# Decayed attention and a GELU MLP in one program: where the loads, the attention steps and the copies of waves 0 to 2 stand, and the last block in two halves

## The chip, the cores and the metric

The kernel runs on one core of a Trainium2 chip. The metric is device time in microseconds (us) of one launch: the median of several runs. One more execution is profiled; its span is the time from the first to the last instruction that the profiler saw.

Engines: PE (TensorE, matmuls into PSUM), DVE (VectorE), ACT (ScalarE), POOL (GpSimd), SP (SyncE, which here only issues DMAs). Each engine works through its own queue in order, and semaphores hold an instruction until what it needs is done. A DMA that SP or POOL issues is carried out by 16 DMA engines that all queues share.

## What is computed

Four sequences of 768 positions, eight heads of 64. In blocks of 64 positions a linear attention with a decay `lam` per head is computed, with a state `kv_state` that goes from block to block; the result, as 3072 rows of 512, goes through a two-layer MLP.

```python
for b in range(nb):                                    # nb = 768 // 64
    intra = np.einsum('bhic,bhjc->bhij', qb, kb) * Dmask[None]
    intra = np.einsum('bhij,bhjd->bhid', intra, vb)
    inter = np.einsum('bhid,bhde->bhie', qb * lam_pow[None], kv_state)
    out[:, :, sl] = intra + inter
    kv_state = lam_block[None, :, None, None] * kv_state + np.einsum('bhsd,bhse->bhde', kb_dec, vb)
...
h = x @ w_in                                           # 512 -> 2048
g = h * (1.0 / (1.0 + np.exp(-1.702 * h)))
return (g @ w_out).astype(np.float32)                  # 2048 -> 512
```

## The kernel before

**Waves.** The work is cut into six waves of 512 rows (`NW` = 6). Waves 0 and 1 are "big": two of the four sequences each, 256 positions at once. Waves 2 to 5 take 128 positions of all four sequences. Heads go in four pairs, p = 0 to 3. A wave's attention gives four tiles `xT` (one for each pair, 128 x 512, bf16), which are the MLP's input, transposed.

**MLP.** `mlp1(w, fc, kcs)` (L371) makes one 128 x 512 tile of the hidden layer out of four matmuls, over the four `xT` tiles, and ACT writes its GELU to `g_sb` (L381). `mlp2(w, g, j)` (L383) makes four of the 16 matmuls of one block of 128 output rows; the last of the four j copies the block on DVE to `o_sb` (L392) and stores it through SP (L394). A call of either is one item of the list `main`, four matmuls with 512 columns each; the first nine items of waves 0 and 1 are cut up differently (three tiles begun on the first two pairs, then one matmul each for the third and the fourth pair).

**Attention of a big wave.** `big_cast` (L219) multiplies k or q by a decay and casts it to bf16, on DVE or POOL as the call says; `big_cast_v` (L227) casts v on POOL; `big_t` (L232) transposes k and q of one pair on PE and copies both out of PSUM on ACT (L242); `big_s` (L245) makes the scores; `big_m` (L259) masks them on DVE (L262); `big_kv` (L268) makes the states of two pairs, which ACT copies to `mid` and `first` (L283, L284); `big_st` (L287) combines them on DVE; `big_c` (L294) makes the output of one pair, and ACT copies it to `xT` (L311).

**Attention of waves 2 to 5.** `do_cast` (L193) scales k and q on DVE (L199, L200), casts v on POOL, and has k and q transposed by a DMA on SP's queue (L205). `scores` (L314) makes the scores of two pairs on PE (L321) and masks them on DVE (L325); `mix` (L348) makes their output and the new state.

**Order.** All engines' orders follow the order in which the program is written out. The prologue up to L474 is written by hand: wave 0's attention, filler matmuls on a tile of zeros between its steps (`fill`, L215), loads of the weights on POOL's queue (`w_in` in five chunks, then `w_out` in four, cast to bf16 on the way), and on SP's queue, behind a wait, the loads of waves 1 and 2. That wait is `sync_behind_weights` (L186): SP copies four bytes out of `w_out_sb[2]`, the third of the four chunks, so that nothing behind it on SP's queue is issued before that chunk has landed. From L475 on, `main` is the list of MLP items of all waves, and `side` is a list of attention steps with due positions: a step is written out ahead of the first item whose index is not below its position (L490 to L494). Wave 0 has items 0 to 37 (22 of `mlp1`, then 16 of `mlp2`, the first eight of them in turns over two blocks, chunk after chunk of `w_out`), wave 1 items 38 to 75. The list `BIG` (L399) gives the positions of wave 1's attention. For a later wave w + 1 they are n + 1 + 2p for the casts and n + `SCORES_AT`, n + `MIX_AT` for scores and mix (L484 to L486), with n = 44 for wave 2.

**PSUM.** Eight banks: three with the tag "mm" (`ps_h`, `ps_out` and, in wave 0, the transposes of `big_t`) and five with the tag "att" (all other attention tiles). `bank(..., mm)` (L209) picks the tag. A tile of a tag waits until the tile that had its buffer has been read.

Of the kernel before, what the change touches and what calls it, by code (L numbers as in the profile page):

```python
# [24 lines left out]
def kernel(  # L25
# [13 lines left out]
    nc = tc.nc  # L39
    f32 = mybir.dt.float32  # L40
    bf16 = mybir.dt.bfloat16
    B, H, S, D = q.shape
    P = 128
# [27 lines left out]
    NB = 2  # L71
# [76 lines left out]

    def more_consts():
        nc.scalar.activation(inv_pow, ln_lam, EXP, scale=i_inv)  # L150
        for h in range(2):
            hs = slice(64 * h, 64 * h + 64)
            nc.scalar.activation(blk_pow[hs], ln_lam[hs].rearrange("p (n h) -> p n h", h=2)[:, :, h], EXP, scale=i_blk[hs])

    def last_consts():
        for x, i in ((k_pow, i_k), (q_pow, i_q)):
            nc.scalar.activation(x, ln_lam, EXP, scale=i)

# [26 lines left out]

    def sync_behind_weights():  # L186

        nc.sync.dma_start(out=behind, in_=w_out_sb[2][0:1, 0, 0:2])


    cast, trans, masked, xT, g_of, h_ps, o_ps, vbig, sc_of, kv_of = ({} for _ in range(10))
# [37 lines left out]
        nc.gpsimd.tensor_copy(vb, pair_of(w, "v", p))  # L229
        vbig[w, p] = vb  # L230

    def big_t(w, p, q_out=None):  # L232
        kq = work.tile([P, 2, BB, 2, P], bf16, tag=f"kq{p}", name="kqB")
        for i, nm in enumerate("kq"):
            ps_t = bank([P, BB, 2, P], bf16, f"ps_t{nm}", w == 0)
            for bb in range(BB):
                for t in range(2):
                    nc.tensor.transpose(ps_t[:, bb, t, :], cast[w, p][:, i, bb, t, :], ident)  # L238
            if nm == "q" and q_out is not None:
                q_out.tensor_copy(kq[:, i], ps_t)  # L240
            else:
                nc.scalar.copy(kq[:, i], ps_t)  # L242
        trans[w, p] = kq
# [127 lines left out]
    def mlp1(w, fc, kcs):  # L371
# [8 lines left out]
        if kcs[-1] == KC - 1:  # L380
            nc.scalar.activation(g_of[w][:, fc, :], h_ps.pop(fc), GELU)  # L381

    def mlp2(w, g, j):  # L383
        if j == 0:
            o_ps[w, g] = ps.tile([P, d_model], f32, tag="mm", bufs=3, name="ps_out")
        ps_out = o_ps[w, g]
        for fc in range(j * CW, (j + 1) * CW):
            nc.tensor.matmul(ps_out, g_of[w][:, fc, g * P : (g + 1) * P], w_out_sb[j][:, fc % CW, :],  # L388
                             start=(fc == 0), stop=(fc == FFC - 1))
        if j == FFC // CW - 1:  # L390
            o = op.tile([P, d_model], f32, tag="o", name="o_sb")
            nc.vector.tensor_copy(o, ps_out)  # L392
            r0 = (BB * w + g // 2) * S + (g % 2) * P if w < NB else g * S + w * P
            nc.sync.dma_start(out=out[r0 : r0 + P, :], in_=o)  # L394

    EARLY = 3
    SCORES_AT, MIX_AT = (13, 21), (19, 27)
    V, G_ = nc.vector, nc.gpsimd
    BIG = [(27, big_cast, "k", 0, V), (27, big_cast, "q", 0, G_), (27, big_cast, "k", 1, V), (27, big_cast, "q", 1, G_),  # L399
           (30.5, big_cast, "k", 2, V), (30.5, big_cast, "k", 3, V), (30.5, big_cast_v, 0), (30.5, big_cast_v, 1),  # L400
           (31, big_t, 0), (32, big_t, 1), (33, big_s, 0), (33, big_m, 0), (34, big_s, 1), (34, big_m, 1),
           (34, big_kv, 0, False), (34, big_st, 0), (34, big_cast, "q", 2, G_), (34, big_cast, "q", 3, V),
           (35.5, big_c, 0), (35.5, big_c, 1), (36.5, big_t, 2), (36.5, big_t, 3), (37, big_s, 2), (37, big_m, 2),
           (37.5, big_s, 3), (37.5, big_m, 3), (37.5, big_cast_v, 2), (37.5, big_cast_v, 3), (38, big_kv, 2, False),
           (41, big_c, 2), (41, big_c, 3, 0, V.tensor_copy), (41, big_st, 2)]
    first, last = list(range(KC - 1)), [KC - 1]

    def mlp2_items(w):

        nj = FFC // CW  # L410
        if w == 0:
            return ([(mlp2, w, g, j) for j in range(nj) for g in range(2)]
                    + [(mlp2, w, g, j) for g in range(2, G) for j in range(nj)])
        return [(mlp2, w, g, j) for g in range(G) for j in range(nj)]

    def mlp_items(w):
# [7 lines left out]
    with tc.manual_schedule():  # L424
# [5 lines left out]
        big_cast(0, "q", 0, G_)  # L430
        big_t(0, 0)
        more_consts()
        last_consts()
        big_cast(0, "k", 1, V)
        big_cast(0, "q", 1, G_)
        big_s(0, 0, 3)
        big_m(0, 0)
        big_t(0, 1)
        nc.scalar.preload_act_table(GELU)
        big_s(0, 1, 2)  # L440
        big_m(0, 1)
# [3 lines left out]
        load_w_in(1)  # L445
        big_kv(0, 0, False, 3)
        big_cast(0, "k", 2, V)
        big_c(0, 0, 6)
        big_c(0, 1, 8)
        big_cast(0, "q", 2, G_)  # L450
        load_w_in(2)
        load_w_in(3)
        big_cast(0, "k", 3, V)
        big_cast(0, "q", 3, V)
        big_st(0, 0)
        big_t(0, 2)
        big_t(0, 3)
        big_s(0, 2, 2)
        big_m(0, 2)
        big_s(0, 3, 1)  # L460
# [15 lines left out]
        for w in range(NW):  # L476
            n = len(main)
            main += mlp_items(w)
            e = len(main)
            if w == 0:  # L480
                side += [(at, (f, 1, *a)) for at, f, *a in BIG]
            elif w + 1 < NW:
                n = e - FFC - len(mlp2_items(w))
                side += [(n + 1 + 2.0 * p, (do_cast, w + 1, p)) for p in range(NP)]  # L484
                for i, ps2 in enumerate(([0, 1], [2, 3])):
                    side += [(n + SCORES_AT[i], (scores, w + 1, ps2)), (n + MIX_AT[i], (mix, w + 1, ps2))]  # L486
            if w and w + 2 < NW:
                side += [(n + 8, (load, w + 2))]
        side.sort(key=lambda x: x[0])
# [35 lines left out]
```

## Time and profile before

| | us |
|---|---|
| median of 3 runs | 218.73 (218.3 to 218.84) |
| the profiled execution | 218.17 |
| its span | 216.5 |
| PE busy in the span | 203.1 |
| ACT, DVE, POOL busy | 87.3, 84.8, 31.9 |
| first w_out matmul of wave 0 on PE | 33.67 |
| last matmul's copy on DVE begins | 212.70 |

A line of the timeline gives start, length, engine, line of the kernel, operation, output and inputs, and how many instructions were merged into it; the bracket is the engine's idle time just before and what ended it. "SPq" is SP issuing DMAs. A line of the chain of waits gives start, length and what the end of the program hung on at that time. In lines of groups, the two numbers behind the bar are the busy time and the mean of one instruction in ns. A line on landing gives the time from the issue of a DMA to its data being there. The PEclk row of the slices is the clock that TensorE was granted, in tenths.

### The profile page before, as it was taken

What the parts mean: (1) busy time and instruction counts of PE and PEld (TensorE: products, weight loads), DVE (VectorE), ACT (ScalarE), POOL (GpSimd) and SP (SyncE); (2) the same over time, 40 slices, a digit from 0 to 9 for tenths busy, and PEclk for the clock granted to TensorE, in tenths of its full rate; (3) what the DMA queues carried; (4) which work ended last, traced back from release to release, by engine and by line L of the source; (5) the groups of instructions that cost most, each with busy time, mean ns of one, the idle gap of its engine ahead of it and who ended that gap; (6) DMA issues with size and microseconds to landing.
All of it is one profiled execution on the core that took longest, in us unless ns stands there. A gap on an engine that the chain in (4) does not pass through costs nothing.

```text
span 216.5 us, 4280 instructions
## 1 busy us (share of the span) xinstructions
PE 203.1 (94%) x1721; PEld 100.5 (46%) x1747; DVE 84.8 (39%) x187; ACT 87.3 (40%) x164; POOL 31.9 (15%) x60
## 2 busy tenths in 40 slices
PE   7789999988897999999999999999999999999992
PEld 2465444545443455444545444545444545444440
DVE  2687000585853173442283533282624061100121
ACT  4784772236664311166311275301366301476000
POOL 3698000442130012100211000111000000000000
PEclk9999999999999999999999999999999999999999
DMA  4999998998999979689992299991390012100112
GB/s 123 291 253 207 202 199 191 290 271 177 211 282 194 196 170 229 219 159 201 227 211 85 97 184 208 201 234 53 107 184 1 3 55 87 55 0 0 48 65 80
DMA packets 88695, 33.83 MB, mean 156 GB/s; under 512 B 68708, under 2 KB 85604, under 8 KB 88676
## 3 DMA queue, kind: packets, MB, share of 16 engines
q1 hardware_dynamic: 83380, 29.11, 56.1%
q0 software_dynamic: 4752, 4.19, 12.1%
q10 hardware_dynamic: 544, 0.26, 0.4%
q8 instruction: 13, 0.21, 0.4%
q14 instruction: 6, 0.05, 0.1%
HBM read 27.27 MB, written 6.29 MB: 155 GB/s over the span
## 4 chain that ended last, share of the span: by engine, by line
PE 73%; DMA 16%; SPq 4%; POOL 2%; issue 2%; ACT 1%; DVE 1%; DVEq 0%
PE ps_out L388 33%; PE ps_h L378 31%; DMA w_out<-in_moe_w_out_dram 7%; DMA qb<-in_q_dram 4%; SPq L96 3%; DMA kb<-in_k_dram 3%; PE ps_o L362 2%; PE ps_o L355 2%; PE ps_s L321 2%; DMA kqT<-kqs 2%; POOL w_in L176 1%; PE ps_kv L338 1%; POOL w_out L180 1%; POOL vb L229 1%; PE ps_o L307 1%
## 5 line engine op out<-in xcount | busy, mean ns | idle before, releaser
L378 PE MATMUL ps_h<-xT,w_in 128*128 128x512 bf16 x375 | 84.4, 379 | 1.7 <-ACT xT L311 0.5
L388 PE MATMUL ps_out<-w_out,g_sb 128*128 128x512 bf16 x368 | 84.2, 379 | 1.7 <-issue 1.4
L381 ACT ACTIVATE g_sb<-ps_h 128x512 bf16<-128x512 f32 x96 | 56.9, 597 | 47.4 <-PE ps_h L378 47.2
L378 PEld LDWEIGHTS <-w_in 128*128 128x128 bf16 x384 | 37.1, 98 | 45.4 <-issue 1.6
L388 PEld LDWEIGHTS <-g_sb 128*128 128x128 bf16 x384 | 36.2, 98 | 42.2
L392 DVE COPY o_sb<-ps_out 128x512 f32<-128x512 f32 x24 | 16.6, 691 | 46.2 <-PE ps_out L388 45.6
L325 DVE SCALAR_TENSOR_TENSOR sm<-ps_s,inv_pow,mask 128x512 bf16<-128x512 f32 x32 | 21.8, 744 | 27.6 <-PE ps_s L321 27.6
L367 ACT CAST xT<-ps_o 128x512 bf16<-128x512 f32 x16 | 8.6, 589 | 43.5 <-PE ps_o L362 43.5
L202 POOL CAST v_sb<-vf 128x512 bf16<-128x512 f32 x16 | 10.5, 656 | 86.8 <-DMA vf<-in_v_dram 73.7
L225 DVE TENSOR_TENSOR kqb<-kb,kb_pow 128x256 bf16<-128x256 f32 x16 | 7.0, 481 | 22.8 <-DMA kb<-in_k_dram 22.8
L345 DVE SCALAR_TENSOR_TENSOR kv<-kv,blk_pow,ps_kv 128x256 bf16<-128x256 bf16 x12 | 5.2, 477 | 23.3 <-PE ps_kv L338 23.3
L262 DVE SCALAR_TENSOR_TENSOR smb<-ps_s,inv_pow,mask_b 128x512 bf16<-128x512 f32 x16 | 11.2, 745 | 5.4 <-PE ps_s L255 4.4
L200 DVE TENSOR_SCALAR kqs<-qf,q_pow 128x256 bf16<-128x256 f32 x32 | 11.1, 348 | 0.6 <-DMA qf<-in_q_dram 0.5
L225 POOL TENSOR_TENSOR kqb<-qb,qb_pow 128x256 bf16<-128x256 f32 x12 | 7.5, 642 | 24.8 <-DMA qb<-in_q_dram 22.1
L199 DVE TENSOR_SCALAR kqs<-kf,k_pow 128x256 bf16<-128x256 f32 x32 | 11.1, 347 | 0.0
L242 ACT COPY kqB<-ps_tk 128x512 bf16<-128x512 bf16 x8 | 4.8, 594 | 9.4 <-PE ps_tk L238 9.4
L321 PE MATMUL ps_s<-kqT 64*128 64x128 bf16 x128 | 5.1, 217 | 1.6 <-DMA kqT<-kqs 1.4
L321 PEld LDWEIGHTS <-kqT 64*128 64x128 bf16 x128 | 3.6, 94 | 5.0 <-issue 2.1
L311 ACT CAST xT<-ps_o 128x256 bf16<-128x256 f32 x12 | 4.4, 454 | 3.4 <-PE ps_o L307 3.4
L217 PE MATMUL fill<-warm 128*128 128x512 bf16 x10 | 4.4, 631 | 1.3 <-DVE i_blk L135 1.3
L238 PEld LDWEIGHTS <-kqb 128*128 128x128 bf16 x64 | 3.9, 98 | 3.4 <-DVE kqb L225 1.6
L355 PEld LDWEIGHTS <-kv 64*64 64x64 bf16 x128 | 3.8, 106 | 3.4 <-issue 3.4
(55 smaller groups left out, 88.0 us busy)
## 6 DMA issues: line engine op xcount, KB each, us to landing
out_dram<-o_sb SPq DMA_DIRECT2D x24, 256.0 KB, 2.0
kf<-in_k_dram SPq DMA_DIRECT2D x32, 128.0 KB, 3.3
qf<-in_q_dram SPq DMA_DIRECT2D x32, 128.0 KB, 3.3
vf<-in_v_dram SPq DMA_DIRECT2D x32, 128.0 KB, 3.4
vb<-in_v_dram SPq DMA_DIRECT2D x8, 256.0 KB, 5.4
w_out<-in_moe_w_out_dram POOLq DMA_DIRECT2D x4, 512.0 KB, 13.6
kb<-in_k_dram SPq DMA_DIRECT2D x6, 256.0 KB, 4.3
qb<-in_q_dram SPq DMA_DIRECT2D x6, 256.0 KB, 5.5
```

What stands on the lines that cost most here:

```text
L199: nc.vector.tensor_scalar(ks[:, :, h, :], kf[:, :, h, :], scalar1=k_pow[:, hd : hd + 1], scalar2=None, op0=MUL)
L200: nc.vector.tensor_scalar(qs[:, :, h, :], qf[:, :, h, :], scalar1=q_pow[:, hd : hd + 1], scalar2=None, op0=MUL)
L202: nc.gpsimd.tensor_copy(v_sb[w % 2][p], vf)
L225: eng.tensor_tensor(x[:, bb].rearrange("p t (h d) -> p h t d", h=2), pair_of(w, nm, p)[:, bb], by, op=MUL)
L262: nc.vector.scalar_tensor_tensor(sm.rearrange("p b t s -> p b (t s)"), s2.rearrange("p b t s -> p b (t s)"), inv_pow[:, 2 * p + h : 2 * p ...
L321: nc.tensor.matmul(s2[p, h][:, b, :], kq[hs, 0, b, :], kq[hs, 1, b, :], start=True, stop=True)
L325: nc.vector.scalar_tensor_tensor(sm, s2[p, h], inv_pow[:, 2 * p + h : 2 * p + h + 1], mask.to_broadcast([P, B, P]), op0=MUL, op1=MUL)
L367: nc.scalar.copy(x, ps_o[p].rearrange("p b s -> p (b s)"))
L378: nc.tensor.matmul(h_ps[fc], w_in_sb[j][:, kc, i * P : (i + 1) * P], xT[w, kc], start=(kc == 0), stop=(kc == KC - 1))
L381: nc.scalar.activation(g_of[w][:, fc, :], h_ps.pop(fc), GELU)
L388: nc.tensor.matmul(ps_out, g_of[w][:, fc, g * P : (g + 1) * P], w_out_sb[j][:, fc % CW, :], start=(fc == 0), stop=(fc == FFC - 1))
L392: nc.vector.tensor_copy(o, ps_out)
```

## The change

Five edits, all of order and of who does what; the computed values are the same.

1. *Prologue.* The constants `blk_pow` move to `last_consts`, which is now written out behind the second pair's `big_t` and ahead of the GELU table load. The first `big_c` has eight fillers for six, the second none for eight. The transposes of pairs 2 and 3 have their q half copied by DVE (`q_out`).
2. *Gate.* SP's wait is on `w_out_sb[1]` for `w_out_sb[2]`.
3. *Wave 1.* New positions in `BIG`; k of pair 3 is cast on POOL for DVE; `big_t` of pairs 2 and 3 have their q half copied by DVE, and that of pair 2 takes "mm" banks. Wave 0's output blocks are copied by ACT for DVE.
4. *Wave 2.* The first `scores` and `mix` come two positions later, the second ones one.
5. *Last block.* The last 128 rows are computed as two blocks of 256 columns by `mlp2_part`, each with its copy on DVE and its store.

```diff
     def more_consts():
         nc.scalar.activation(inv_pow, ln_lam, EXP, scale=i_inv)
+
+    def last_consts():
         for h in range(2):
             hs = slice(64 * h, 64 * h + 64)
             nc.scalar.activation(blk_pow[hs], ...)
-
-    def last_consts():
         for x, i in ((k_pow, i_k), (q_pow, i_q)):
...
-        nc.sync.dma_start(out=behind, in_=w_out_sb[2][0:1, 0, 0:2])
+        nc.sync.dma_start(out=behind, in_=w_out_sb[1][0:1, 0, 0:2])
...
-    def big_t(w, p, q_out=None):
+    def big_t(w, p, q_out=None, mm=None):
...
-            ps_t = bank([P, BB, 2, P], bf16, f"ps_t{nm}", w == 0)
+            ps_t = bank([P, BB, 2, P], bf16, f"ps_t{nm}", w == 0 if mm is None else mm)
...
+    def out_rows(w, g):
+        return (BB * w + g // 2) * S + (g % 2) * P if w < NB else g * S + w * P
...
-            nc.vector.tensor_copy(o, ps_out)
-            r0 = (BB * w + g // 2) * S + (g % 2) * P if w < NB else g * S + w * P
+            (nc.scalar.copy if w == 0 else nc.vector.tensor_copy)(o, ps_out)
+            r0 = out_rows(w, g)
...
+    def mlp2_part(w, g, c0, n):
+        ps_out = bank([P, n], f32, "ps_part", True)
+        for fc in range(FFC):
+            nc.tensor.matmul(ps_out, g_of[w][:, fc, g * P : (g + 1) * P], w_out_sb[fc // CW][:, fc % CW, c0 : c0 + n],
+                             start=(fc == 0), stop=(fc == FFC - 1))
+        o = op.tile([P, n], f32, tag="o", name="o_part")
+        nc.vector.tensor_copy(o, ps_out)
+        r0 = out_rows(w, g)
+        nc.sync.dma_start(out=out[r0 : r0 + P, c0 : c0 + n], in_=o)
...
-           (30.5, big_cast, "k", 2, V), (30.5, big_cast, "k", 3, V), (30.5, big_cast_v, 0), (30.5, big_cast_v, 1),
-           (31, big_t, 0), (32, big_t, 1), (33, big_s, 0), (33, big_m, 0), (34, big_s, 1), (34, big_m, 1),
-           (34, big_kv, 0, False), (34, big_st, 0), (34, big_cast, "q", 2, G_), (34, big_cast, "q", 3, V),
-           (35.5, big_c, 0), (35.5, big_c, 1), (36.5, big_t, 2), (36.5, big_t, 3), (37, big_s, 2), (37, big_m, 2),
-           (37.5, big_s, 3), (37.5, big_m, 3), (37.5, big_cast_v, 2), (37.5, big_cast_v, 3), (38, big_kv, 2, False),
-           (41, big_c, 2), (41, big_c, 3, 0, V.tensor_copy), (41, big_st, 2)]
+           (27, big_cast_v, 0), (27, big_cast_v, 1), (30, big_t, 0), (31, big_t, 1), (31, big_s, 0), (31, big_m, 0),
+           (32, big_s, 1), (32, big_m, 1), (32, big_cast, "k", 3, G_), (32, big_cast, "k", 2, V),
+           (34, big_kv, 0, False), (34, big_cast, "q", 2, G_), (34, big_cast, "q", 3, V), (34, big_st, 0),
+           (35, big_c, 0), (35, big_c, 1), (35.5, big_t, 2, V, True), (36, big_t, 3, V),
+           (36.5, big_s, 2), (36.5, big_m, 2), (37, big_s, 3), (37, big_m, 3), (37, big_cast_v, 2), (37, big_cast_v, 3),
+           (38, big_kv, 2, False), (41, big_c, 2), (41, big_c, 3, 0, V.tensor_copy), (41, big_st, 2)]
...
+        if w == NW - 1:
+            return ([(mlp2, w, g, j) for g in range(G - 1) for j in range(nj)]
+                    + [(mlp2_part, w, G - 1, c0, d_model // 2) for c0 in (0, d_model // 2)])
...
         more_consts()
-        last_consts()
...
         big_t(0, 1)
+        last_consts()
...
-        big_c(0, 0, 6)
-        big_c(0, 1, 8)
+        big_c(0, 0, 8)
+        big_c(0, 1)
...
-        big_t(0, 2)
-        big_t(0, 3)
+        big_t(0, 2, V)
+        big_t(0, 3, V)
...
-                    side += [(n + SCORES_AT[i], (scores, w + 1, ps2)), (n + MIX_AT[i], (mix, w + 1, ps2))]
+                    at = 2 - i if w == 1 else 0
+                    side += [(n + SCORES_AT[i] + at, (scores, w + 1, ps2)), (n + MIX_AT[i] + at, (mix, w + 1, ps2))]
```

## The prediction, made before the changed kernel was built or run

> **What bounds the kernel now.** I read the shares and slices of the page first, then the chain of waits, then TensorE's own timeline.
>
> ```profile
> span 216.5 us, 4280 instructions
> PE 203.1 (94%) x1721; PEld 100.5 (46%) x1747; DVE 84.8 (39%) x187; ACT 87.3 (40%) x164; POOL 31.9 (15%) x60
> PE   7789999988897999999999999999999999999992
> PEclk9999999999999999999999999999999999999999
> ```
>
> TensorE (PE) is busy throughout and its granted clock is full, so only holes in its work can be closed. From slice 14 on (75.8 us) there are none to speak of: a steady wave is solid matmul. What can be won lies before 70 us and behind the last matmul. The chain:
>
> ```profile
> 19.04 14.62 DMA w_out<-in_moe_w_out_dram
> 33.68 0.75 SPq L188
> 38.99 5.71 DMA kb<-in_k_dram
> 45.74 0.76 DVE smb L262
> 65.28 3.90 DMA kqT<-kqs
> 212.70 0.69 DVE o_sb L392
> ```
>
> The third w_out chunk lands at 33.66 and only then does SP begin to issue the loads of wave 1; their last k tile (5.71 us in flight) holds VectorE, which holds a mask multiplication, which holds PE; later the transposes of wave 2 hold PE. PE's own timeline (start, length, then the idle time before in brackets) shows where it paid:
>
> ```profile
> 33.67 7.93 PE L388 MATMUL ps_out<-w_out,g_sb 128*128 128x512 bf16 x35
> 41.44 0.39 PE L238 MATMUL ps_tk<-ident,kqb 128*128 128x128 bf16 x4
> 46.54 0.44 PE L279 MATMUL ps_kv<-vb,kqb 64*64 64x64 bf16 x30 [0.63 <-DVE smb L262]
> 52.19 0.42 PE L255 MATMUL ps_s<-kqB 64*64 64x128 bf16 x16 [0.49 <-ACT kqB L242]
> 56.91 1.46 PE L378 MATMUL ps_h<-xT,w_in 128*128 128x512 bf16 x6 [0.27 <-ACT xT L311]
> 68.05 0.40 PE L321 MATMUL ps_s<-kqT 64*128 64x128 bf16 x8 [0.64 <-DMA kqT<-kqs]
> 69.23 0.40 PE L321 MATMUL ps_s<-kqT 64*128 64x128 bf16 x8 [0.78 <-DMA kqT<-kqs]
> ```
>
> Removable: 0.63 + 0.49 in wave 1's attention, 0.64 + 0.78 = 1.42 at wave 2's first scores. The pitch of a 512-column matmul is (41.44 - 33.67) / 36 = 0.216 us, so one item of the main list (four matmuls) takes 0.863 us, and item 22 + n of wave 0 starts at 33.67 + 0.863 n.
>
> **Part 1, the prologue.** Three constants move behind the second pair's transposes, six filler matmuls go, the q halves of two transposes are copied by VectorE.
>
> ```profile
> 10.10 1.28 ACT L439 ACT_TABLE_LOAD   x1
> 11.41 0.76 ACT L283 CAST mid<-ps_kv 64x256 bf16<-64x256 f32 x2
> 12.78 1.05 PE L217 MATMUL ps_o<-warm 128*128 128x256 bf16 x8
> 13.67 0.28 PE L299 MATMUL ps_o<-kqB,mid 128*128 128x128 bf16 x2
> 15.59 0.38 PE L238 MATMUL ps_tq<-ident,kqb 128*128 128x128 bf16 x4 [0.53 <-ACT kqB L242]
> ```
>
> ScalarE's table load runs right into mid (10.10 + 1.28 = 11.38), and it had no idle time since the first pair's copies. With the constants moved it waits some 0.45 us for the second pair's transposes and has the constants still to do, so the table load, mid and the first big_c come about 0.45 later (an estimate from these rows); without its eight fillers (12.78 to 13.67, 0.11 each, 0.89 us) the second big_c still ends about 0.2 earlier. The 0.53 us wait of the last transposes is on a PSUM buffer that the k copy frees, about 15.4 instead of 15.59; the q copies on VectorE (as 0.69 us, from the 512-column copy below) end at 16.0 and 16.7, against 16.0 and 17.0 on ScalarE. I take -0.15 us for the whole; bounds -0.5 (nothing delayed but the copies faster) and +0.4 (the 0.45 us delay comes through).
>
> **Part 2, the gate.** SP waits for the second chunk of w_out, not the third.
>
> ```profile
> L180 POOL DMA_DIRECT2D w_out<-in_moe_w_out_dram x2: 762/766/770, 18.3 to 19.0; - x2
> DMA to landing us min/median/max: 12.7/13.6/14.6
> L180 POOL DMA_DIRECT2D w_out<-in_moe_w_out_dram x2: 770/774/777, 19.0 to 19.8; - x2
> DMA to landing us min/median/max: 14.6/15.5/16.4
> 34.60:35.40 0.80, 0.80 (x6) 0.33 (x5) 0.00 (x0) 0.00 (x0) 0.00 (x0) 1.00 0.45 81
> 35.40:36.20 0.80, 0.80 (x5) 0.39 (x4) 0.00 (x0) 0.00 (x0) 0.00 (x0) 1.00 0.40 101
> 36.20:37.40 1.20, 1.20 (x8) 0.55 (x6) 0.00 (x0) 0.00 (x0) 0.00 (x0) 1.00 1.11 328
> 37.40:38.40 1.00, 1.00 (x6) 0.43 (x5) 0.23 (x1) 0.00 (x0) 0.00 (x0) 1.00 0.63 171
> ```
>
> Chunk 1 (counted from 0) lands at 18.3 + 12.7 = 31.0, chunk 2 at 33.7, chunk 3 at 19.8 + 16.4 = 36.2. SP's first load goes out 2.7 us earlier, and behind SP's wait stand all loads of waves 1 and 2, then the stores of wave 0 and the transposes of wave 2: all move with it as far as the DMA engines let them. In these rows of the stretches view the last two columns are the mean busy share of the DMA engines and GB/s. The share is 0.45 and 0.40 for 1.6 us, and 0.63 for 1 us after 37.4, against 1.11 when full. Filled, these holes are worth 1.6 x 0.6 + 1.0 x 0.43 = about 1.4 us. But the thin 34.6 to 36.2 is the tail of chunk 3 on the engines that are last; on those there is no hole, and a load has landed only when all engines are done. So the loads come between 0.4 us (the second hole alone) and 2.0 us earlier. I take 0.5 for the ones that wave 1 waits for, since a load lands with its last engine.
>
> Chunk 3 itself is needed by item 28, at 33.67 + 6 x 0.863 - 0.15 = 38.7. In the old run the first load is issued 0.8 us after the gate, and the rate rises about 0.9 us after that (the row from 35.40); so the new loads' data begin at about 31.0 + 1.7 = 32.7, with 36.2 - 32.7 = 3.5 us of w_out work left on the last engines. How long that takes beside the loads hangs on w_out's share of an engine:
>
> ```profile
> q0 software_dynamic: 408, 0.40, 122.7%
> q1 hardware_dynamic: 1201, 0.60, 121.2%
> ```
>
> These are two stretches of 2 us, one all w_out (28 to 30), one all loads (42 to 44): 2 x 16 x 1.227 / 408 = 96 ns a w_out packet, 2 x 16 x 1.212 / 1201 = 32 ns a load packet; taken in turn w_out has 96 / 128 = 75%. With 60 to 75% it lands between 37.4 and 38.5: no wait, which I take; at an even share at 39.7: 1.0 us. The Trainium skill, "DMA: Bandwidth & Descriptors", section "Queues, rings and completion order", says that an engine goes round its queues a whole packet at a time. By that rule w_out keeps its 75% and chunk 3 is safe, but the early loads gain less, which speaks against placing wave 1's steps earlier: the first wait below would be nearer 0.75 than 0.5, and the sum 217.0.
>
> **Part 3, wave 1's steps.** The first transposes move from item 31 to 30, scores to 31 and 32, and the second half's k casts behind both masks, so that late k loads hold neither VectorE nor the kv step: -0.63. A whole item now stands between the second half's transposes and their scores, with half of the four copies on VectorE: -0.49. Against that stand four new waits.
>
> ```profile
> 41.02 1.76 POOL L225 TENSOR_TENSOR kqb<-qb,qb_pow 128x256 bf16<-128x256 f32 x3 [0.45 <-DMA qb<-in_q_dram]
> L381 ACT ACTIVATE g_sb<-ps_h 128x512 bf16<-128x512 f32 x96 | 56.9, 597 | 47.4 <-PE ps_h L378 47.2
> ```
>
> First: GpSimd's second q cast starts when its load lands, at 41.02, and ends 0.6 us later, 41.63. The first q transpose is now due at 41.44 - 0.86 - 0.15 + 0.22 = 40.65. With loads 0.5 us earlier PE waits about 0.5 us, with loads 2 us earlier not at all, with loads not earlier 1.0; I take 0.5. Second: wave 0's stores are copied by ScalarE now (0.60 us each), and one (item 33) ends just before the kv step's mid copies, so these start about 0.2 us late, and big_c now follows one item after kv: I take +0.2 (0 to 0.35). Third: the second pair's transposes take two of the three "mm" PSUM buffers, so wave 1's first ps_h may have to wait for the copy of wave 0's last block: 0.2 + 0.60 us after it, less the 0.44 us of kv step and its switch: 0.4; no row shows which buffer is given, so 0 to 0.4, and I take 0.3. Fourth: chunk 3, above, 0 (0 to 1.0). The 0.27 at 56.91 stays. Sum of parts 2 and 3: -1.12 + 0.5 + 0.2 + 0.3 = -0.12 (from -1.1 to +1.6).
>
> **Part 4, wave 2's steps.** Its first scores and mix come two items later (1.73 us of PE work), the second ones one item later.
>
> ```profile
> 75.86 1.07 ACT L367 CAST xT<-ps_o 128x512 bf16<-128x512 f32 x2 [2.91 <-PE ps_o L362]
> 76.45 1.67 PE L388 MATMUL ps_out<-w_out,g_sb 128*128 128x512 bf16 x7 [0.16 <-issue]
> ```
>
> The last transpose needed lands at 65.28 + 3.90 = 69.2. The new scores reach PE at 68.05 - 0.64 + 1.73 - 0.15 - 0.12 = 68.9, their second half 0.27 later at 69.1; with transposes 0.4 us earlier, 68.8, neither waits: -1.42. Were the transposes not earlier, 0.1 remains. The second scores then follow the first mix by one item, at 76.45 + 0.86 = 77.3 in old time, when ScalarE's copies that free their PSUM are done (75.86 + 1.07 = 76.9): 0. Bounds -1.42 and -0.4 (GpSimd or VectorE later by 1 us).
>
> **Part 5, the end.** The last 128 rows are computed in two halves of 256 columns.
>
> ```profile
> L392 DVE COPY o_sb<-ps_out 128x512 f32<-128x512 f32 x24 | 16.6, 691 | 46.2 <-PE ps_out L388 45.6
> L311 DVE CAST xT<-ps_o 128x256 bf16<-128x256 f32 x4 | 1.6, 442 | 1.7 <-PE ps_o L307 1.7
> out_dram<-o_sb SPq DMA_DIRECT2D x24, 256.0 KB, 2.0
> ```
>
> PE: 32 matmuls at the fillers' 0.11 us are 3.52 us against 16 x 0.216 = 3.46: +0.06; the fillers have a weight load each too, so the doubled weight loads are covered. The last copy takes 0.44 instead of 0.69: -0.25. The store of 128 KB for 256 KB: between 0 and -0.5 off the 2.0 us; I take -0.1. The first half's copy and store lie under the second half's 1.75 us of matmuls. Sum -0.3 (0 to -0.7).
>
> **The sum.** -0.15 - 0.12 - 1.42 - 0.3 = -2.0. The profiled execution took 218.17 us (1.67 around its span), the runs' median is 218.73, 0.56 above it. On the median: 218.73 - 2.0 = 216.7. About 0.3% (0.65 us) is what a measurement can tell here.
>
> **Rivals.**
> A, the loads really come 2 us earlier. For it: the mean DMA share of 0.4 after 34.6. Against: the tail of chunk 3. The first wait goes and the PSUM buffer is a free one: 216.7 - 0.5 - 0.3 = 215.9.
> B, wave 1 eats its gain: loads not earlier (1.0), mid 0.35, buffer 0.4, the prologue 0 and chunk 3 0.3 late: -1.12 + 2.05 - 1.42 - 0.3 = -0.8, so 217.9. For it: every new wait hangs on work that the trace has within 0.3 us of its due time.
> C, the slower side: w_out loses the DMA engines. If the loads, with 12 x 0.26 MB queued, take two thirds of each engine, 3.5 us of w_out become 10.5: chunk 3 lands at 43.2, not by 38.7, and all PE work stands behind it, since items 28 and on need it and wave 1's attention is in order behind them. 4.5 - 0.5 (the first wait, covered) - 2.0 = +2.0: 220.7; at 60% for the loads, 8.75 us and 41.45, 218.9. It decides from a landing at about 41.2. Against: the packet times.
> D, PE's clock falls in the thinner prologue. The first fillers run at half pace:
>
> ```profile
> L217 PE MATMUL fill<-warm 128*128 128x512 bf16 x10 | 4.4, 631 | 1.3 <-DVE i_blk L135 1.3
> ```
>
> 631 ns against 379 for a warm one; 16 matmuls at half pace cost 16 x 0.216 = 3.5 us: 220.2. Against: holes of up to 0.76 us stand in the old prologue at full clock, and the new ones are no longer than about 1.2.
>
> **How the numbers follow.** Forecast 0.44 (216.7, own range 216.1 to 217.4), A 0.20, B 0.20 (217.9, reaching to 218.6), C 0.12, D 0.04. Range 215.3 to 218.8: below A by the unknown ends of the prologue and the store, above B by part of C's lower end. Faster by over 0.3% is the forecast, A and most of B: 0.77; within 0.3%: the rest of B and a mild C, 0.09; slower 0.14.
>
> **What would show it.** Right: no kqT wait before the wave 2 scores, no smb wait at the kv step, a q cast on GpSimd that starts at about 40.5, a last VectorE copy near 0.44 us. Wrong: a wait of ps_out on w_out (C), PE idle before the first ps_h of wave 1 well over 0.4 us, or a second w_out wait of SP elsewhere; if the scores of wave 2 still wait for kqT, the load stream did not move.

## The result, and the profile after

| | before | changed |
|---|---|---|
| median of 4 runs, us | 218.51 (218.07 to 218.84) | 215.59 (215.14 to 215.79) |
| ratio, 95% interval | | 0.9865 (0.9839 to 0.989) |
| the profiled execution, us | 218.17 | 215.14 |
| its span, us | 216.5 | 213.4 |

The kernel became 2.9 us faster (2.4 to 3.5 by the interval); 2.0 was forecast. 215.59 lies inside the stated range (215.3 to 218.8) but below the forecast's own range (216.1 to 217.4), and nearest to rival A's 215.9. Runs more than 1.5% above the fastest of their kernel are left out of all ratios here, but not out of the medians. The page of the changed kernel, its span, PE's slices and granted clock, and the shares of the chain of waits by engine:

```profile
span 213.4 us, 4323 instructions
PE   7779999999999999999999999999999999999994
PEclk9999999999999999999999999999999999999999
PE 91%; DMA 4%; DVE 1%; ACT 1%; POOL 1%; SPq 0%; issue 0%; POOLq 0%
```

The same row of shares before:

```profile
PE 73%; DMA 16%; SPq 4%; POOL 2%; issue 2%; ACT 1%; DVE 1%; DVEq 0%
```

The slices between 43 and 60 us that had an 8 and the one at 65 us that had a 7 are full; one in the prologue went from 8 to 7. DMAs are down from 16% of the chain to 4%. PE's timeline after, at the places that the prediction showed (start, length, then idle before):

```profile
33.90 7.07 PE L391 MATMUL ps_out<-w_out,g_sb 128*128 128x512 bf16 x32
41.02 0.44 PE L238 MATMUL ps_tq<-ident,kqb 128*128 128x128 bf16 x4
46.20 0.45 PE L279 MATMUL ps_kv<-vb,kqb 64*64 64x64 bf16 x32
51.46 0.64 PE L255 MATMUL ps_s<-kqB 64*64 64x128 bf16 x32
53.38 1.47 PE L378 MATMUL ps_h<-xT,w_in 128*128 128x512 bf16 x6
56.15 1.46 PE L378 MATMUL ps_h<-xT,w_in 128*128 128x512 bf16 x6 [0.27 <-ACT xT L311]
68.31 0.62 PE L321 MATMUL ps_s<-kqT 64*128 64x128 bf16 x16
69.73 4.48 PE L391 MATMUL ps_out<-w_out,g_sb 128*128 128x512 bf16 x20
```

All four waits that were to go are gone: the kv step is one row of 32 matmuls without a bracket, so are the second half's scores (32) and wave 2's first scores (16). To see where the time came from I cut each span at five marks: the first w_out matmul of wave 0 (33.67 before, 33.90 now), the row with the wait for xT in wave 1 (56.91, 56.15), wave 1's first w_out matmul (72.16, 69.73), the start of the last copy (212.70, 210.32), the end.

| stretch, us | before | changed | difference | forecast |
|---|---|---|---|---|
| prologue and wave 0's first layer | 33.67 | 33.90 | +0.23 | -0.15 |
| wave 1's attention | 23.24 | 22.25 | -0.99 | -0.12 |
| wave 1's first layer, wave 2's first scores | 15.25 | 13.58 | -1.67 | -1.42 |
| from there to the last copy | 140.54 | 140.59 | +0.05 | +0.06 (part 5) |
| last copy and store | 3.80 | 3.08 | -0.72 | -0.36 (part 5) |

### The profile page after: what moved, and what is told of

Read it like the earlier page. It is cut to its first block, busy times and chain, and to the rows that moved or that the text cites. A ratio compares the mean times of both kernels' runs of the same rounds, so it can differ in the third digit from the quotient of the medians.

```text
span 213.4 us, 4323 instructions
## 1 busy us (share of the span) xinstructions
PE 204.8 (96%) x1757; PEld 101.1 (47%) x1757; DVE 83.8 (39%) x186; ACT 87.4 (41%) x164; POOL 33.2 (16%) x62
## 4 chain that ended last, share of the span: by engine, by line
PE 91%; DMA 4%; DVE 1%; ACT 1%; POOL 1%; SPq 0%; issue 0%; POOLq 0%
PE ps_h L378 39%; PE ps_out L391 38%; DMA vb<-in_v_dram 2%; PE ps_o L362 2%; PE ps_o L355 2%; PE ps_s L321 2%; PE ps_part L402 2%; DMA qb<-in_q_dram 2%; PE ps_o L307 1%; PE ps_s L255 1%; PE ps_kv L279 1%; PE ps_kv L338 1%; ACT xT L311 1%; PE ps_tq L238 1%; ACT g_sb L381 1%; POOL vb L229 1%
## 5 line engine op out<-in xcount | busy, mean ns | idle before, releaser
L378 PE MATMUL ps_h<-xT,w_in 128*128 128x512 bf16 x384 | 85.3, 379 | 1.1 <-ACT xT L311 0.5
L391 PEld LDWEIGHTS <-g_sb 128*128 128x128 bf16 x368 | 34.5, 98 | 40.2
L395 DVE COPY o_sb<-ps_out 128x512 f32<-128x512 f32 x19 | 13.1, 691 | 47.0 <-PE ps_out L391 46.6
L225 DVE TENSOR_TENSOR kqb<-kb,kb_pow 128x256 bf16<-128x256 f32 x14 | 6.3, 492 | 19.7 <-DMA kb<-in_k_dram 17.1
L395 ACT COPY o_sb<-ps_out 128x512 f32<-128x512 f32 x4 | 2.3, 585 | 10.4 <-PE ps_out L391 10.4
L229 POOL CAST vb<-vb 128x512 bf16<-128x512 f32 x8 | 4.7, 616 | 3.3 <-DMA vb<-in_v_dram 3.2
```

The source lines that it names most:

```text
L225: eng.tensor_tensor(x[:, bb].rearrange("p t (h d) -> p h t d", h=2), pair_of(w, nm, p)[:, bb], by, op=MUL)
L378: nc.tensor.matmul(h_ps[fc], w_in_sb[j][:, kc, i * P : (i + 1) * P], xT[w, kc], start=(kc == 0), stop=(kc == KC - 1))
L395: (nc.scalar.copy if w == 0 else nc.vector.tensor_copy)(o, ps_out)
```

## The experiments

Each group of four ran on one chip beside the kernel before, which took a median of 219.2, 219.4 and 219.45 us there, with runs from 217.6 to 222.4; so ratios to it are compared, each good to 0.3 to 0.5%, 0.7 to 1.1 us. Finer differences are read from the marks in the profiles.

**e5: the changed kernel again.** No edit.

> The changed kernel itself, unaltered, beside the next three on one chip, as the measure for them. Theory (what differs between runs is when the DMAs land, and the changed kernel has 0.1 to 0.3 us to spare at its two DMA-bound steps, the first q transpose of wave 1 and the first scores of wave 2): the median is within 0.5 us of 215.6, and a profile with later loads shows waits at just these two steps. Rival (the gain of 2.9 was a lucky set of runs): 216.5 or more.

216.33 us, ratio 0.9864 (0.9814 to 0.9914): the first ratio again, so the gain is no luck, though the 216.33 itself is 0.74 above 215.59, outside the 0.5 of the expectation; the kernel before was as much higher there. PE in its profile:

```profile
41.82 0.28 PE L238 MATMUL ps_tq<-ident,kqb 128*128 128x128 bf16 x2 [0.19 <-POOL kqb L225]
69.64 0.40 PE L321 MATMUL ps_s<-kqT 64*128 64x128 bf16 x8 [0.29 <-DMA kqT<-kqs]
```

With loads some 0.6 us later than in the first profile of the changed kernel, waits show at just the two DMA-bound steps: there is next to no slack at either.

**e1: the gate put back.**

```diff
-        nc.sync.dma_start(out=behind, in_=w_out_sb[1][0:1, 0, 0:2])
+        nc.sync.dma_start(out=behind, in_=w_out_sb[2][0:1, 0, 0:2])
```

> The changed kernel with only the gate put back on the third w_out chunk. In the changed kernel's profile the first load's data landed 5.2 us after its issue at 32.70, only 0.3 us earlier than before, although the gate opened 1.8 us earlier; GpSimd's q cast that waits for its load began at 40.51 against 41.02. Theory (a load lands with its last DMA engine, so the gate is worth about 0.5 us): the loads come about 0.5 us later again, PE waits about 0.6 us at wave 1's first q transpose (the cast then ends near 41.6, due 41.0), the transposes of wave 2 come later by as much as PE does, so no new wait there: about 0.5 us slower than the changed kernel, 216.1, and still 2.4 faster than before. Rival (the gate pays by its whole 2.7 us or the mean DMA holes of 1.4 to 2.0 us): PE waits 1.5 to 2 us, 217.1 to 217.6.

217.39 us, ratio 0.9916 (0.9881 to 0.9951). In its profile PE waits twice for late loads:

```profile
41.29 0.28 PE L238 MATMUL ps_tq<-ident,kqb 128*128 128x128 bf16 x2 [0.52 <-POOL kqb L225]
69.63 0.40 PE L321 MATMUL ps_s<-kqT 64*128 64x128 bf16 x8 [0.82 <-DMA kqT<-kqs]
```

The first wait is the one that the theory gave (0.6 expected). The second it had ruled out. From the first w_out matmul to the last copy PE needs 211.42 - 33.37 = 178.05 against 210.32 - 33.90 = 176.42, 1.6 us more in this pair of profiles; against e5's, 211.43 - 34.23 = 177.20, it is 0.85, and the ratios of the two kernels (0.9916, 0.9864) are 1.1 us apart, with intervals that overlap. So the gate is worth some 1 to 1.6 us in this order of steps, toward the rival's size, in two waits rather than one. My theory on the gate's size fell, because it had the kqT landings move with PE. They did not: PE was 0.65 us earlier in wave 1 than before (56.26 for 56.91 at the row with the wait for xT), and the first transpose was still issued 30.0 us after the gate (63.54 - 33.50) for 29.9 before (63.56 - 33.68).

**e7: the gate on the first chunk.**

```diff
-        nc.sync.dma_start(out=behind, in_=w_out_sb[1][0:1, 0, 0:2])
+        nc.sync.dma_start(out=behind, in_=w_out_sb[0][0:1, 0, 0:2])
```

> The changed kernel with SP's wait on the first w_out chunk, so that the loads may start some 2.6 us earlier still. From the gate to the first cast it took 4.4 to 4.5 us with the third chunk as the gate and 6.0 to 6.2 with the second. Theory (w_out keeps most of each DMA engine as long as it runs, so a load issued early waits behind it): gate to first cast about 8 us, the first k cast near 37.3 to 37.9 again, the fourth w_out chunk in time, total within 0.4 us of the changed kernel. Rival C of the prediction (the loads take the engines from w_out): the fourth chunk lands late and PE waits more than 0.5 us ahead of the seventh w_out item of wave 0, due at 38.9, and the total is at least 0.5 us above the changed kernel. Rival A (more time, more gain): loads 1 us or more earlier than in the changed kernel, no waits for DMA left, 215.2.

216.25 us, ratio 0.9841 (0.9789 to 0.9893), no different from the changed kernel. SP's four-byte DMA, which starts when the gate opens, the first k cast, and PE from wave 0's first w_out matmul, in e7's timeline:

```profile
29.71 0.75 SPq L188 DMA_DIRECT2D behind<-w_out  x1
38.23 0.43 DVE L225 TENSOR_TENSOR kqb<-kb,kb_pow 128x256 bf16<-128x256 f32 x1 [15.72 <-DMA kb<-in_k_dram]
34.40 7.07 PE L391 MATMUL ps_out<-w_out,g_sb 128*128 128x512 bf16 x32
```

The same two rows of the changed kernel and of e1:

```profile
31.91 0.75 SPq L188 DMA_DIRECT2D behind<-w_out  x1
37.90 0.43 DVE L225 TENSOR_TENSOR kqb<-kb,kb_pow 128x256 bf16<-128x256 f32 x1 [15.90 <-DMA kb<-in_k_dram]
```

```profile
33.50 0.75 SPq L188 DMA_DIRECT2D behind<-w_out  x1
37.91 0.42 DVE L225 TENSOR_TENSOR kqb<-kb,kb_pow 128x256 bf16<-128x256 f32 x1 [16.44 <-DMA kb<-in_k_dram]
```

Gate to first cast: 8.5 us with chunk 0, 6.0 with chunk 1 (6.0 to 6.3 in all nine profiles with that gate), 4.4 with chunk 2 (3.8 to 4.5 in four). Chunks land some 2.6 us apart. So, counted from the landing of w_out, the first step back brings the loads 2.6 - 1.6 = 1.0 us forward, the second 2.6 - 2.5 = 0.1: the hole behind w_out seems to be filled by then. All 32 w_out matmuls of e7's row run in 7.07 us without a wait, as in the changed kernel: the prediction's rival C is refuted even one chunk earlier. The fourth chunk landed 18.6 us after its issue at 20.0, so at 38.6, against 37.1 in the changed kernel (17.0 after 20.1), and its item was due at 34.40 + 6 x 0.863 = 39.6: 1.0 us was left.

**e10: the gate alone**, in the kernel before (the edit of the change).

> The kernel before with the gate alone moved to the second chunk. Theory (the gate brings the load stream some 1.0 to 1.3 us forward on w_out's own clock; e1 without it was slower by about 1.4 us in two waits): the smb wait falls from 0.63 to about 0.4, the kqT waits from 1.42 to 0.5 or less, in all 1.0 to 1.4 us less than before. Rival (w_out holds the engines, so an earlier gate brings nothing, as e7 against the changed kernel): within 0.3 us of before.

217.68 us, ratio 0.992 (0.9888 to 0.9952): 1.8 us less than the kernel before beside it, somewhat more than expected. Its profile took 217.95, and the expected fall of the kqT waits is not in it:

```profile
46.41 0.44 PE L279 MATMUL ps_kv<-vb,kqb 64*64 64x64 bf16 x30 [0.28 <-DVE smb L262]
68.98 0.40 PE L321 MATMUL ps_s<-kqT 64*128 64x128 bf16 x8 [0.80 <-DMA kqT<-kqs]
```

The smb wait fell from 0.63 to 0.28, the first kqT wait from 0.64 to 0.51; the second stayed at 0.80. The gate opened at 31.72 there, and the first cast began at 37.98, just 0.19 earlier than before. That the gate alone gains is measured; where the rest of it comes from in a typical run this one profile doesn't show.

**e3: wave 2's steps put back; e11: these steps alone**, in the kernel before (the edit of the change).

```diff
-                    at = 2 - i if w == 1 else 0
+                    at = 0
```

> The changed kernel with wave 2's scores and mix at their old positions. In the changed kernel the two transposes that the first scores need landed at 62.7 + 4.6 = 67.3 and 64.7 + 3.7 = 68.4. At the old positions the scores are due near 66.6 and 66.85. Theory (the two items are worth the whole wait): PE waits for kqT about 0.7 and then 0.8, the sum 1.5 to 1.7 us, 217.1 to 217.3. Rival (the earlier loads had already taken the wait away): at most 0.9 us, 216.5 or less.

216.74 us, ratio 0.9872 (0.982 to 0.9924), with runs from 215.58 to 219.10: by times alone not to be told from the changed kernel; the 217.1 to 217.3 of the theory did not show. Its profile is of the longest run, with q loads 2 us late (GpSimd's second q cast began at 42.61 for 40.51 in the changed kernel); the kqT waits in it:

```profile
69.76 0.40 PE L321 MATMUL ps_s<-kqT 64*128 64x128 bf16 x8 [1.02 <-DMA kqT<-kqs]
70.76 0.40 PE L321 MATMUL ps_s<-kqT 64*128 64x128 bf16 x8 [0.60 <-DMA kqT<-kqs]
```

The stretch is 73.69 - 58.25 = 15.44 us against 13.58, but with loads that late it is no clean measure; so I also ran the other half.

> The kernel before with wave 2's scores and mix alone at the new positions. Theory (before, PE reaches the scores 1.5 to 1.7 us ahead of kqT, and two items are 1.73 us): kqT waits of 0 to 0.3 us left, the stretch from wave 1's second part to its first w_out matmul 13.6 to 13.9 us for 15.25, 1.3 to 1.7 us less than before in all. Rival (the wait moves to the masks and the mix, which are due two items later but have the same work): less than 0.8 us gained, with PE idle ahead of the mix.

218.14 us, ratio 0.9954 (0.9916 to 0.9991), 1.0 us less than before. Its scores come without a wait:

```profile
70.47 0.62 PE L321 MATMUL ps_s<-kqT 64*128 64x128 bf16 x16
71.90 4.48 PE L388 MATMUL ps_out<-w_out,g_sb 128*128 128x512 bf16 x20
```

The stretch is 71.90 - 58.31 = 13.59 us, as in the changed kernel (13.58) and against 15.25 before: two items take the whole wait away, and nothing comes back at the mix (71.90 to the last copy at 212.44 is 140.54, as before). The margin is small: the second transpose that the scores need landed at 66.4 + 4.0 = 70.4, and their second half was due at 70.7. In time the gain is less than the 1.3 to 1.7 us expected, perhaps because other runs have other waits.

**e2: wave 1's steps put back; e12: these steps alone.** For e2 the list `BIG` and the copies of wave 0's blocks are as before; e12 is the kernel before with these two as changed.

```diff
-            (nc.scalar.copy if w == 0 else nc.vector.tensor_copy)(o, ps_out)
+            nc.vector.tensor_copy(o, ps_out)
...
-           (27, big_cast_v, 0), (27, big_cast_v, 1), (30, big_t, 0), (31, big_t, 1), (31, big_s, 0), (31, big_m, 0),
...
+           (31, big_t, 0), (32, big_t, 1), (33, big_s, 0), (33, big_m, 0), (34, big_s, 1), (34, big_m, 1),
```

> The changed kernel with the old positions, engines and banks of wave 1's attention, and wave 0's blocks copied on VectorE; gate, prologue, wave 2 positions and last block as changed. Theory (the steps themselves are worth about 1.0 us, the difference of the two profiles between wave 0's first w_out matmul and wave 1's second stretch): the smb wait at the kv step and the kqB wait at the second half's scores come back, 0.8 to 1.2 us slower than the changed kernel, 216.4 to 216.8; with the loads 0.3 to 0.5 us earlier the smb wait is shorter than 0.63. Rival (the earlier gate alone would have removed the smb wait): only the kqB wait of about 0.5 comes back, 216.1, and the kv step starts without a wait.

215.86 us, ratio 0.9838 (0.9798 to 0.9878): no dearer than the changed kernel by the times, where 0.8 to 1.2 us more was expected. In its profile both old waits are back, the smb wait shorter, as expected:

```profile
46.51 0.44 PE L279 MATMUL ps_kv<-vb,kqb 64*64 64x64 bf16 x30 [0.41 <-DVE smb L262]
52.16 0.42 PE L255 MATMUL ps_s<-kqB 64*64 64x128 bf16 x16 [0.49 <-ACT kqB L242]
```

Its stretch is 56.88 - 33.44 = 23.44 against 22.25 in the changed kernel, 1.2 more in that run. With the steps as changed it was 22.56 in e5, 22.89 in e1, but also 23.36 in e6 and 24.88 in e3, with its late loads, so it moves between runs by as much as the steps should bring.

> The kernel before with wave 1's steps, engines and banks alone as changed (and wave 0's blocks copied by ScalarE). Theory (kqT lands when the load stream lets it, whatever PE does before; PE gained in wave 1 waits at the scores): the smb and kqB waits are gone, a q transpose waits 0.5 to 0.8 us, what is won comes back as a longer kqT wait, in all within 0.3 us of before. Rival (the parts add up): 0.6 to 1.0 us less than before.

219.15 us, ratio 0.9988 (0.9958 to 1.0018): nothing gained, the size that the theory had. PE in its profile:

```profile
41.60 0.28 PE L238 MATMUL ps_tq<-ident,kqb 128*128 128x128 bf16 x2 [0.63 <-POOL kqb L225]
42.79 0.28 PE L238 MATMUL ps_tq<-ident,kqb 128*128 128x128 bf16 x2 [0.90 <-POOL kqb L225]
68.75 0.40 PE L321 MATMUL ps_s<-kqT 64*128 64x128 bf16 x8 [0.23 <-DMA kqT<-kqs]
70.13 0.40 PE L321 MATMUL ps_s<-kqT 64*128 64x128 bf16 x8 [0.98 <-DMA kqT<-kqs]
```

The smb and kqB waits are gone, but the time came back elsewhere than the theory had it: at the q transposes, 1.5 us in two waits for GpSimd's casts, and not at kqT, where PE waits 0.23 + 0.98 = 1.21 for 1.42 before. The gate opened 1.2 us later in this run than in the profile before (34.88 for 33.68); counted from it, PE reaches the row with the wait for xT after 58.02 - 34.88 = 23.14 us, and after 56.91 - 33.68 = 23.23 before. The earlier steps pay nothing without the earlier loads.

**e4: the last block in one piece.**

```diff
-        if w == NW - 1:
-            return ([(mlp2, w, g, j) for g in range(G - 1) for j in range(nj)]
-                    + [(mlp2_part, w, G - 1, c0, d_model // 2) for c0 in (0, d_model // 2)])
```

> The changed kernel with the last 128 rows as one block again. The profiles have 3.8 us from the start of the last copy to the end of the span before, 3.1 with two halves. Theory (the shorter copy 0.27, the landing 2.0 against 1.7, and the rest): 0.6 to 0.7 us slower than the changed kernel, 216.2 to 216.3. Rival (only the copy is shorter, the end of the span differs from run to run by as much): 0.25 us, 215.85.

215.65 us, ratio 0.9843 (0.98 to 0.9887). The times can't tell: the 0.6 to 0.7 us more that was expected is within their error and did not show. The marks can. Its span, its last copy, and the last copy of the changed kernel:

```profile
span 213.6 us, 4287 instructions
209.88 0.69 DVE L395 COPY o_sb<-ps_out 128x512 f32<-128x512 f32 x1 [2.76 <-PE ps_out L391]
```

```profile
210.32 0.42 DVE L405 COPY o_part<-ps_part 128x256 f32<-128x256 f32 x1 [1.32 <-PE ps_part L402]
```

From the last copy's start to the end: 3.72 us in e4, 3.80 before, 3.74 in e10, 3.76 in e11, 3.79 in e12; with two halves 3.08, and 3.07 to 3.18 in six others. By these marks the two halves are worth 0.6 us, more than the shorter copy (0.27).

**e6: the old prologue.** The order of the constants, the fillers and the copies up to the second half's transposes of wave 0 are as before.

```diff
-        big_c(0, 0, 8)
-        big_c(0, 1)
+        big_c(0, 0, 6)
+        big_c(0, 1, 8)
...
-        big_t(0, 2, V)
-        big_t(0, 3, V)
+        big_t(0, 2)
+        big_t(0, 3)
```

> The changed kernel with the old prologue: blk_pow, k_pow and q_pow ahead of the second pair's transposes, 6 and 8 fillers, all q halves copied by ScalarE. Wave 0's first w_out matmul stood at 33.67 before; with the new prologue it stood at 33.90 in the changed kernel's profile and at 33.29 to 33.44 in four others. Theory (the new prologue is worth about 0.25 us, the 33.90 was a late load): that matmul at about 33.65 and 0.2 to 0.3 us more in all, 215.9. Rival (it is worth nothing or costs time, as the pair of profiles has it): at 33.3 to 33.5 and no more time than the changed kernel.

215.67 us, ratio 0.9825 (0.9783 to 0.9867); wave 0's first w_out matmul at 34.02:

```profile
34.02 7.07 PE L391 MATMUL ps_out<-w_out,g_sb 128*128 128x512 bf16 x32
```

Inconclusive. With the old prologue this mark stands at 33.67 to 34.03 in five profiles, mean 33.84; with the new one at 33.29 to 34.40 in nine, mean 33.69. A difference of 0.15 in the mean is small against that spread, and e6's time shows no loss.

**e8 and e9: further on.** e8 moves wave 2's steps two items more and cuts the last block into 384 and 128 columns; e9 adds one item for wave 1's first steps and casts pair 0's q on VectorE.

```diff
-                    at = 2 - i if w == 1 else 0
+                    at = 4 - i if w == 1 else 0
...
-                    + [(mlp2_part, w, G - 1, c0, d_model // 2) for c0 in (0, d_model // 2)])
+                    + [(mlp2_part, w, G - 1, 0, 3 * P), (mlp2_part, w, G - 1, 3 * P, P)])
...
-           (27, big_cast_v, 0), (27, big_cast_v, 1), (30, big_t, 0), (31, big_t, 1), (31, big_s, 0), (31, big_m, 0),
+           (27, big_cast_v, 0), (27, big_cast_v, 1), (31, big_t, 0), (31, big_t, 1), (32, big_s, 0), (32, big_m, 0),
...
```

The first two edits are in both; the last, of which one line is shown, is e9's alone.

> The changed kernel with wave 2's first scores and mix two items later still, the second ones two items later too, and the last block in parts of 384 and 128 columns. Theory (a wait for kqT remains in runs with late loads, and the end hangs on the last copy and store): no wait for kqT in any profile, the last copy about 0.3 us for 0.42, 0.2 to 0.5 us less than the changed kernel in the median, 215.2, and less spread. Rival (the scores are late enough, and a mix so near the next wave makes PE wait for xT): equal or up to 0.5 us slower, with a wait ahead of wave 2's first ps_h.

> The kernel of e8 with wave 1's first steps one item later (transposes of both pairs ahead of item 31, scores ahead of 32 and 33) and q of pair 0 cast on VectorE behind both k casts, q of pair 1 on GpSimd at the same time. In e8 the only wait for a DMA left was 0.32 us at the first q transpose; in seven profiles of the changed order the q cast began between 40.1 and 42.6. Theory (slack of one item, 0.86 us, and a cast of 0.42 for 0.61 at the late end take that wait away; nothing else hangs on it): no wait at the q transposes, 0.2 to 0.4 us under e8, about 214.9, and less spread upward. Rival (the kv step and the outputs then wait for masks or for ScalarE's copies): a wait of 0.3 us or more ahead of the scores or of big_c, no gain over e8 (215.1).

e8: 215.14 us, ratio 0.9805 (0.9758 to 0.9851); e9: 215.43, 0.9823 (0.9777 to 0.9869). e8's span and last copy:

```profile
span 213.1 us, 4323 instructions
210.27 0.29 DVE L405 COPY o_part<-ps_part 128x128 f32<-128x128 f32 x1 [0.34 <-PE ps_part L402]
```

2.83 us from the last copy to the end, 0.25 less than with halves, and no kqT wait; a wait of 0.32 us at the first q transpose is left. e8's median is 1.2 us under e5's on the same chip, but the intervals of the two ratios overlap. e9 shows no wait for a DMA at the q transposes or the scores, yet no gain over e8; perhaps the last waits in question were too short and too rare to show.

## Why the prediction was right, and where its sizes were off

**What bounds the kernel.** As forecast: a solid stream on PE from wave 1's first w_out matmul to the last copy (140.5 to 140.6 us in every profile but those of e8 and e9, where it begins elsewhere), so all of the gain lies before that matmul (72.16 before, 69.73 now) and behind the last one.

**Part 1, the prologue.** Forecast -0.15. The pair of profiles has +0.23, the means of all profiles -0.15. The mark moves by 1.1 us between runs of one prologue, so this term is not settled. Two waits of the changed prologue in its profile:

```profile
11.00 0.32 PE L279 MATMUL ps_kv<-vb,kqb 64*64 64x64 bf16 x16 [0.62 <-POOL vb L229]
15.76 0.38 PE L238 MATMUL ps_tq<-ident,kqb 128*128 128x128 bf16 x4 [0.62 <-DVE kqB L240]
```

The first came with a late load of v. The second stands where the old prologue waited 0.53 for ScalarE's k copy, a wait that was to shrink by about 0.2; it is now for VectorE's q copy, which began only at 15.29, behind other work of that engine.

**Part 2, the gate.** What held: an earlier gate yields less than its 2.7 us, and chunk 3 was in no danger. That this is because a load lands with its last engine is not shown by these runs. GpSimd's second q cast began where the prediction put it, 41.02 - 0.5 = 40.52:

```profile
40.51 1.75 POOL L225 TENSOR_TENSOR kqb<-qb,qb_pow 128x256 bf16<-128x256 f32 x3 [0.21 <-DMA qb<-in_q_dram]
```

But this 0.5 was partly chance, since chunk 1 landed at 31.9, not 31.0, in that execution; counted from the landing of w_out the gate gives 1.0 us (e1, e7). In time it gives about as much or more: 1.8 us alone (e10), some 1 to 1.6 us in the changed order (e1). The share of the engines was wrong too, see the last section: w_out kept nearly all of them, not 60 to 75%, and its last chunk landed 5.2 us after chunk 1 (37.1, 31.9), just as before (36.2, 31.0).

**Part 3, wave 1: the term farthest off in the profiles.** Forecast -0.12, measured -0.99 in this pair of profiles, where three waits had been charged with 1.0 us and 0.16 came. The first (0.5): PE's q transpose was due at 40.65 by the sum and at 41.02 in the run, since the prologue came later, while the cast ended near 41.1. So there was no slack to speak of: 0.19 of wait in e5, 0.52 in e1. That it did not show here is luck. The second (0.2) came nearly as put: big_c starts 1.02 us after the item ahead of it for 0.86. The third (0.3) did not come:

```profile
53.10 0.58 ACT L395 COPY o_sb<-ps_out 128x512 f32<-128x512 f32 x1 [2.00 <-PE ps_out L391]
```

Wave 1's first ps_h starts at 53.38 while ScalarE copies wave 0's last block until 53.68: it does not wait for that block's buffer. And the two waits removed were larger than their brackets (the next part says how): the kv step took 1.20 us from 45.72 and takes 0.38, and in the second half the scores, which began about 0.65 after the end of their transposes' issue, follow a whole item instead, so nearly 1.5 went for 1.12. Of that, about 0.3 came back in small gaps, some 0.1 each, where PE goes from 512-column matmuls to the small ones of scores and kv, at more places than before:

```profile
43.05 1.04 PE L391 MATMUL ps_out<-w_out,g_sb 128*128 128x512 bf16 x4
44.02 0.42 PE L255 MATMUL ps_s<-kqB 64*64 64x128 bf16 x16
```

Four matmuls of 0.216 are 0.863 us; the scores come 0.97 after their start.

The times don't confirm the -0.99: wave 1's steps alone bring nothing (e12, 0.9988), and without them the kernel is no slower (e2, 0.9838; e5, with them, 0.9864). So over several runs the term may well be near the -0.12 of the forecast; what it is worth beside the earlier gate is not settled.

**Part 4, wave 2's scores.** Forecast -1.42, measured -1.67, and e11 shows it alone (13.59 for 15.25). The mis-sizing is in how a bracket was read: it counts from the modelled end of the last matmul, while the matmuls of a stream start 0.216 apart, before that end. Before, 40 matmuls of 0.216 from 58.61 end their issue at 67.24, and the scores started at 68.05: 0.81 lost for a bracket of 0.64; the second half (0.27 after 68.05) started at 69.23: 0.91 for 0.78. The sum is 1.72.

**Part 5, the end.** Forecast -0.3, measured -0.6 to -0.7. The copy was sized rightly (0.42 for the 0.44 taken, against 0.69). The store was not:

```profile
L407 SPq DMA_DIRECT2D out_dram<-o_part x2: 333/333/333, 209.0 to 210.8; - x2
DMA to landing us min/median/max: 1.7/1.7/1.7
```

It lands 1.7 us after its issue for 2.0, and of the 0.72 some 0.15 are left that lie behind the landing; I had taken 0.1 for all of the store.

**The parts together.** Alone, the gate gives 0.992, wave 2's steps 0.9954, wave 1's steps 0.9988; with 0.6 of 218.5 us for the end, 0.9973, the product is 0.984, against 0.9865 and 0.9864 for all, within the error. By these the gate and wave 2's steps carry it. Taken out one at a time, only the gate stands out in the times (e1, 0.9916); e2, e3, e4 and e6, at 0.9825 to 0.9872, are not to be told from the changed kernel. So the gate is shown by both, and wave 2's steps by e11 and by the marks.

Rivals: A has the nearest time, but not by its mechanism. The loads were not 2 us earlier (the first k cast began at 37.90 for 38.17); the first wait did not show and the buffer was a free one, for other reasons, and parts 4 and 5 were larger than forecast. Of B's waits the first came in e5 and e1; C's did not come. D's half pace did not come: behind the first fillers, which run at 584 ns for 631 before, the other 128x512 matmuls of the prologue take 379 to 380 ns, as before.

## What to carry to other kernels

Place a step that waits for a DMA by the landing, with some slack for how far it moves from run to run (the first k cast began between 36.96 and 38.79 in the nine profiles with the gate on chunk 1), and not by the engine ahead of it: time won earlier on that engine can be lost again at the next load, as in e12. A gate that holds loads behind a bulk transfer is worth moving only as long as the loads come earlier for it: here by 1.0 us for the first chunk and 0.1 for the second. Where nothing follows, at the very end, cutting the last block in two leaves a shorter copy and a shorter store behind the last matmul, here 0.6 us less.

## What the runs showed of the hardware that was not expected

Loads issued while the w_out DMAs were running got almost nothing of the DMA engines. In the changed kernel the first load was issued at 32.70; between 34.0 and 35.2 the queues' shares were:

```profile
q0 software_dynamic: 233, 0.23, 115.4%
q1 hardware_dynamic: 39, 0.02, 5.8%
```

In e7, with the first load issued at 30.50, between 31.7 and 32.9 w_out's queue alone has a row, and between 32.9 and 34.1:

```profile
q0 software_dynamic: 248, 0.25, 123.3%
q1 hardware_dynamic: 5, 0.00, 0.7%
```

So there were 2.4 us in e7 (31.7 to 34.1) in which loads had been issued and hardly a packet of them ran, where two queues in turn would have given them a quarter by the packet times of the prediction. The Trainium skill, "DMA: Bandwidth & Descriptors", section "Queues, rings and completion order", has engines go round the queues packet by packet; this trace doesn't show that while w_out has work, and what held the loads back is not settled by these runs.

In the changed prologue VectorE copied 128x512 of bf16 out of PSUM in about 0.41 us, where the prediction took the 0.69 us of the f32 copy:

```profile
15.29 0.41 DVE L240 COPY kqB<-ps_tq 128x512 bf16<-128x512 bf16 x1
```
